# A fused attention and two-MoE kernel on one core: weight conversions on a timetable, second-MoE weights begun later, first stage reordered, state update ahead of output

## The chip, the cores and the metric

The kernel runs on one core of a Trainium2 chip. The metric is the time of one execution on the device, in microseconds (us). Other times here are us too, unless marked ns. The five engines of the core each work through their own list of instructions in order: TensorE (PE in the profile; its weight loads are PEld), VectorE (DVE), ScalarE (ACT), GpSimd (POOL) and SyncE (SP, which here issues nearly all transfers).

## The reference

```python
# attention: B, H, S, D = 4, 8, 768, 48
for t in range(S):
    state = alpha[:, :, t, :, None] * state + np.einsum('bhd,bhe->bhde', k[:, :, t], v[:, :, t])
    y[:, :, t] = np.einsum('bhd,bhde->bhe', q[:, :, t], state)
# x: 3072 tokens x 384
rms = np.sqrt(np.mean(x * x, axis=-1, keepdims=True) + 1e-06)
xn = x / rms * rms_g
g = xn @ w_gate                      # 384 x 1536
silu = g * (1.0 / (1.0 + np.exp(-g)))
x = (silu * (xn @ w_val)) @ w_out    # MoE 1
h = x @ w_in                         # 384 x 2048
out = (h * np.cos(h)) @ w_out2       # MoE 2
```

All is float32.

## The kernel before, in words

**Tiles and stages.** The 3072 tokens are cut into 8 blocks of 384 (`TT`). A block has four attention units, one per pair of heads (`units`, 32 in all; the pairs come in the order 3, 0, 1, 2). A unit is scanned (`att_prep`, five VectorE steps: `G`, a reciprocal `dr`, `q*G`, the backward scan, `k` scaled), transposed on PE (`att_T`, matrix `pt`, copied to `th` by ACT), scored (`att_sc0` or `att_sc`, matrices `ps`, copied by ACT and masked by POOL), and then updates the carried state (`att_u`: matrix `pu` needs `th`; VectorE makes `w` from it in three steps, L403 and L407) and gives its output (`att_y`: matrix `py`; the result goes to `xT`). The two last pairs' rows are put into their places by six small copies on SP (`att_fix`, L443 and L444). Then come the squares (`square`, `sq`), their sums over rows on PE (`rms_rows`, `rm`), nine VectorE steps for the inverse root (`rms_inv`, `ny` to `yb`), its spreading on PE (`rms_out`, `rb`, and `y`), and the split of the normed block into a high and a low part (`x_split` or `xn_write`, `xh` and `xl`).

**MoE 1** runs over 12 feature blocks `f` of 128 for each token block: nine matmuls for the gate (`m1_gate`, `pg`), Silu on ACT (`th<-pg`, L649), nine for the value (`m1_val`, `pv`), a product, and `hh` and `hl`, its high and low part; two feature blocks later nine matmuls add to the output (`m1_out`, `o`). Every matrix product takes three matmuls, high by high, high by low and low by high (`mm9`, L611). `pg` and `pv` share three buffers of PSUM, so the third such matrix must wait until the first has been read. For the first block the gate is multiplied by the inverse root afterwards (L647); for the others the input is already normed. MoE 2 follows with 6 blocks of 512 tokens and 16 feature blocks.

**Weights.** They arrive as 64-bit words' halves and must be converted: ACT takes two passes over the raw words (`assemble`, L166 and L168), VectorE joins them (`cv`, L169), ACT makes the high part (`split`, L78), VectorE the low part (L81). The weights of MoE 1 (`st_g`, `st_v`, `st_o` of 768 columns, later `ws` of 384) are converted during the first stage (pieces `a` and `b` of the string `FIRST`) and in the first token block, by `slot()`, which is called three times in each feature block and counts them in `step`. The weights of MoE 2 are loaded into three `ws` buffers (`pre2_stage`), converted from the second token block on (`pre2_conv`) and put back to memory.

**Order.** The work of the first stage is written out by `FIRST`: `p` prepares a unit, `T` transposes, `s` scores, `u` is the state update, `y` the output, `r` squares and row sums, `x` the split, `g` and `v` the first gate and value products, `n` and `o` the inverse root, `i` idle matmuls, `l` loads. Later attention is cut into pieces that a list (`stream`) hands out by `step`. The framework's scheduler then orders each engine's list; `tc.issue_after(x)` keeps what is inside from going ahead of instruction `x`, and `keep_in_program_order` holds an instruction in the place it was written. `slot()` ties a conversion to the Silu and the low part of the feature block before the last (`th_ins[-2]`, `hl_ins[-2]`), and the attention pieces to the end of the first stage (`held`):

```python
        if step[0] < 36 and (step[0] % 3 < 2 or step[0] > 12):
            a = th_ins[-2] if len(th_ins) > 1 else held[0][0]
            d = hl_ins[-2] if len(hl_ins) > 1 else held[0][1]
            with tc.issue_after(a), tc.issue_after(d):
                conv_piece()
            if 1 < streamed[0] and step[0] < NHOLD:
```

Of the kernel before, what the change touches and what calls it, by code (L numbers as in the profile page):

```python
# [42 lines left out]
WS = 2.0 ** 8  # L43
RSQRT_SEED = float(0x5F3759DF)
FIRST = (
    "p0 p1 T0 s0 u0 i3 p2 T1 s1 y0 u1 p3 T2 s2 y1 a0 u2 T3 s3 b0 a1 y2 l4 r0 r1 u3 b1 a2 x0 x1 y3 x2 "
    "g0 r2 b2 n0 v0 g1 o0 v1"
)


@with_exitstack
def fused_kernel(ctx: ExitStack, tc: tile.TileContext, akq, vin, wg, wv, wo, g_in, w2i, w2o, out):
# [100 lines left out]
    def done(eng, ins):  # L153
        mark[eng] = ins.ins
# [5 lines left out]
                st.enter_context(tc.issue_after(x))  # L160
            yield

    def assemble(st, v, pin=False):
        w = st.bitcast(I32).rearrange("p (n t) -> p n t", t=2)
        lo, hi = w[:, :, 0], w[:, :, 1]
        act.activation(out=lo, in_=lo.bitcast(U32), func=AF.Identity, scale=LOW_SCALE, bias=low)  # L166
        g = hi.bitcast(F32)
        done("act", act.activation(out=g, in_=g, func=AF.Prelu, scale=HIGH_SCALE, alpha=NEG_SCALE))  # L168
        ins = dve.scalar_tensor_tensor(  # L169
            out=v, in0=hi, scalar=3, in1=lo, op0=ALU.logical_shift_left, op1=ALU.bitwise_or  # L170
        )
        done("dve", ins)
        if pin:
            tc.keep_in_program_order(ins)
# [39 lines left out]
    def pre2_conv():  # L214
        if not pre2:
            return
        key, q, st = pre2.pop(0)
        if q == 0:
            w2s[key] = [dpool.tile([128, 1536], F32, name=f"d_{key}{x}") for x in "hl"]
        w = cv.tile([128, 2, 384], F32R, tag="whl", name="whl")  # L220
        h, l = w[:, 0, :], w[:, 1, :]
        v = cv_tile(st)
        assemble(st, v, True)
        split(h, l, v.bitcast(F32))
        for x, d in zip((h, l), w2s[key]):
            sp.dma_start(out=d[:, q * 384:(q + 1) * 384], in_=x.bitcast(F32))
        pre2_stage()
# [185 lines left out]
    def att_y(u):  # L413
        i, p = units[u]
        s = un[u]
        py = (ps_a if i else ps_g).tile([128, 512], F32, tag="a" if i else "g", name="py")
        cs = [slice(n * C, (n + 1) * C) for n in range(NB)]
        for n, c in enumerate(cs):
            for r0, r1, j in ((0, 64, 0), (64, R, 1)):
                pe.matmul(py[r0:r1, c], s["v"][:, n, r0:r1], s["s"][:, n, j, :], start=n == 0, stop=False)  # L420
        for n, c in enumerate(cs):
            if n >= 1 - i % 2:
                for r0 in (0, 64):
                    r = slice(r0, r0 + D)
                    done("pe", pe.matmul(  # L425
                        py[r, c], s["st"][n][r, :], s["q"][r, c], start=False, stop=n == NB - 1
                    ))
        if i not in xT:
            xT[i] = m1.tile([128, 4, TT], F32, tag="xT", name="xT")
        x = xT[i]  # L430
        if i:
            act.activation(out=x[:R, p, :], in_=py[:R, :TT], func=AF.Copy)
        else:
            done("act", act.activation(out=x[0:D, p, :], in_=py[0:D, :TT], func=AF.Copy))
            if u == 3:
                done("dve", dve.tensor_copy(out=x[64:R, p, :], in_=py[64:R, :TT]))
            else:
                done("act", act.activation(out=x[64:R, p, :], in_=py[64:R, :TT], func=AF.Copy))

    def att_fix(i):  # L440
        x = xT[i]
# [62 lines left out]
    def rms_out(i):  # L504
        yb = rms.pop(i)
        pb = ps_a.tile([128, 512], F32, tag="a", name="rb")
        done("pe", pe.matmul(pb[:, :TT], ones, yb.rearrange("p a c -> p (a c)"), start=True, stop=True))
        if i == 0:
            y = cv.tile([128, 2, TT], F32, tag="whl", name="y0")[:, 0, :]
        else:  # L510
            y = m1.tile([128, TT], F32, tag="y", name="y")
        done("act", act.activation(out=y, in_=pb[:, :TT], func=AF.Copy))
        rms[i] = y

    def rms_mm(i):
        rms_rows(i, 0, 1)
# [28 lines left out]
    def att_pieces(i):  # L545
# [8 lines left out]
                att_fix(i)  # L554

        if i == 0:
            def sums(c):
                square(0, c)
                rms_rows(0, c, 3)

            fn = dict(
                p=att_prep, T=att_T, s=att_sc0, u=att_u, y=y, a=lambda _: conv_a(), b=lambda _: conv_b(),
                x=x_split, r=sums, i=lambda n: keep_clock(n, ones), l=load_all,
                g=lambda f: pre_gate(f), v=lambda f: pre_val(f), n=lambda _: rms_inv(0), o=lambda _: rms_out(0),
            )
            return [(lambda k=k: fn[k[0]](int(k[1]))) for k in FIRST.split()]
# [13 lines left out]
                att_prep(u + 1)  # L580

        def E(u):
            y(u)
            if u + 1 < len(units):
                att_u(u + 1)
            if u + 2 < len(units):
                att_loadq(u + 2)
                att_loadv(u + 2)
# [26 lines left out]
                k += 1  # L615

    hid1 = {}
    th_ins = []
    hl_ins = []
    acc1 = {}  # L620

    pre = {}
# [17 lines left out]
    def m1_gate(i, f):  # L640
        if i == 0 and f < 2:
            pg = pre.pop(("g", f))
        else:
            pg = m1_mm(i, "g", f, ps_g.tile([128, 512], F32, tag="g", name="pg"))
        p = pg[:, :TT]
        if i == 0:
            dve.tensor_tensor(out=p, in0=p, in1=rms[0], op=ALU.mult)  # L647
        t = m1.tile([128, TT], F32, tag="t", bufs=4, name="th")
        th_ins.append(act.activation(out=t, in_=p, func=AF.Silu, scale=1.0 / WS).ins)  # L649
        return t  # L650

    def m1_val(i, f, t):
# [5 lines left out]
        hh = m1.tile([128, TT], F32R, tag="hh", bufs=3, name="hh")  # L658
        hl = m1.tile([128, TT], F32R, tag="hl", bufs=3, name="hl")
        dve.tensor_tensor(out=p, in0=t, in1=p, op=ALU.mult)  # L660
        copy_r(hh, p)
        hl_ins.append(sub_r(dve, hl, p, hh).ins)
        hid1[i, f] = (hh, hl)

    def m1_out(i, f):
# [276 lines left out]
```

## Time and profile before

| | |
|---|---|
| median of 3 runs | 1025.6 us (1021.43 to 1025.95) |
| the profiled execution | 1024.08 us |
| its span, first to last instruction | 1022.3 us |
| PE busy | 999.3 us, 98% of the span, 5870 matmuls |
| DVE, ACT, POOL busy | 533.9 us (52%), 559.7 us (55%), 178.1 us (17%) |
| mean granted clock of TensorE | 0.984 of full speed |
| chain of work that ended last | PE 92%, DMA 4%, DVE 2%, ACT 1% |

The span is the distance from the first to the last instruction of the profiled execution; 1.8 us of its own time lie around it. The busy shares are means over stages that differ: the first 41 us are attention and the conversion of the first weights, up to 125 us the first token block with the other conversions, up to about 570 us seven blocks of MoE 1 with attention beside them, and the rest is MoE 2. The granted clock is 1.00 at full speed (2.4 GHz) and 0.50 at half (1.2 GHz); a mean between them says how the stretch is shared. "Idle before" names what ended an engine's wait.

### The profile page before, as it was taken

The numbers are of one execution on the slowest core, as the hardware profiler recorded it, in microseconds if no ns is written. First come the engines' busy times: TensorE is split into PE (matmuls) and PEld (weight loads), VectorE is DVE, ScalarE is ACT, GpSimd is POOL, SyncE is SP. The second block draws the span as 40 slices with busy tenths as digits, with TensorE's granted clock in tenths as the row PEclk, the third lists the DMA queues.
The fourth block names the chain that finished last, engine by engine and source line by source line (L and its number), as shares of the span: only waits on it lengthen the run. The fifth ranks groups of instructions, "written<-read, shape, count | busy, mean of one in ns | idle before, by whom it ended". The sixth has DMA issues, their size and how long they took to land.

```text
span 1022.3 us, 15511 instructions
## 1 busy us (share of the span) xinstructions
PE 999.3 (98%) x5870; PEld 883.7 (86%) x5870; DVE 533.9 (52%) x1012; ACT 559.7 (55%) x1089; POOL 178.1 (17%) x189
## 2 busy tenths in 40 slices
PE   8799799999999999999999999999999999999998
PEld 6588799999999999999999998888888888888886
DVE  6879766666567666666625224343343333423333
ACT  4887545555455554554523226565575665755654
POOL 3010010000010000110000122233332233323331
PEclk7799899999999999999999999999999999999999
DMA  8736233343343353343311465010010000000000
GB/s 247 266 117 185 86 104 97 99 139 97 112 143 91 100 160 95 101 134 91 122 49 40 161 253 188 1 31 31 1 63 1 1 31 1 31 1 1 32 1 31
DMA packets 42795, 90.33 MB, mean 88 GB/s; under 512 B 5584, under 2 KB 25552, under 8 KB 42720
## 3 DMA queue, kind: packets, MB, share of 16 engines
q1 hardware_dynamic: 40416, 76.76, 24.5%
q0 software_dynamic: 2304, 12.58, 3.4%
q8 instruction: 46, 0.75, 0.3%
q14 instruction: 29, 0.24, 0.1%
HBM read 66.12 MB, written 22.02 MB: 86 GB/s over the span
## 4 chain that ended last, share of the span: by engine, by line
PE 92%; DMA 4%; DVE 2%; ACT 1%; SPq 0%; issue 0%; DVEq 0%; ACTq 0%
PE p L611 20%; PE ph L611 20%; PE o L611 15%; PE pv L611 14%; PE pg L611 14%; PE py L420 2%; DMA ak<-akq 2%; PE py L425 2%; PE pu L397 1%; DMA q<-akq 1%; PE ps L331 1%; PE ps L332 1%; PE ps L333 1%; DMA st_o<-wo 1%; PE pt L341 1%; PE ps L384 1%
## 5 line engine op out<-in xcount | busy, mean ns | idle before, releaser
L81 POOL TENSOR_TENSOR hl<-kk,hh 128x512 fp32r<-128x512 f32 x93 | 120.1, 1294 | 271.4 <-PE ph L611 105.8
L721 DVE SCALAR_TENSOR_TENSOR kk<-kk,ph 128x512 f32<-128x512 int32 x96 | 66.0, 688 | 142.4 <-ACT kk L720 141.7
L348 POOL TENSOR_SCALAR_AFFINE_SELECT sm<-sm 128x512 f32<-128x512 f32 (+1 forms) x64 | 45.4, 715 | 476.4 <-ACT sm L347 476.4
L724 DVE SCALAR_TENSOR_TENSOR kk<-kk,ph 128x512 f32<-128x512 f32 x96 | 65.9, 687 | 110.7 <-ACT kk L723 110.7
L660 DVE TENSOR_TENSOR pv<-th,pv 128x384 f32<-128x384 f32 x96 | 53.6, 558 | 78.1 <-PE pv L611 54.7
L720 ACT ACTIVATE kk<-ph 128x512 int32<-128x512 f32 x96 | 57.5, 599 | 65.7 <-PE ph L611 48.5
L649 ACT ACTIVATE th<-pg 128x384 f32<-128x384 f32 x96 | 46.7, 487 | 69.4 <-PE pg L611 64.2
L722 ACT ACTIVATE kk<-kk 128x512 f32<-128x512 f32 x96 | 60.6, 631 | 43.5 <-DVE kk L721 42.3
L78 ACT ACTIVATE hh<-kk 128x512 fp32r<-128x512 f32 x96 | 60.5, 631 | 42.9 <-DVE kk L724 38.1
L78 ACT ACTIVATE hh<-pv 128x384 fp32r<-128x384 f32 x96 | 46.9, 488 | 57.0 <-DVE pv L660 56.6
L81 DVE TENSOR_TENSOR hl<-pv,hh 128x384 fp32r<-128x384 f32 x96 | 53.3, 555 | 38.9 <-ACT hh L78 37.9
L723 ACT ACTIVATE kk<-kk 128x512 f32<-128x512 f32 x96 | 60.5, 630 | 2.4
L166 ACT ACTIVATE ws<-ws,low 128x384 int32<-128x384 uint32 x44 | 28.5, 649 | 54.8 <-DMA ws<-w2o 25.4
L78 ACT ACTIVATE bdh<-q 48x384 fp32r<-48x384 f32 x48 | 25.1, 523 | 40.5 <-DVE q L308 39.9
L308 DVE TENSOR_TENSOR q<-q,G 112x384 f32<-112x384 f32 x30 | 16.9, 564 | 42.2 <-DMA q<-akq 42.2
L611 PE MATMUL pv<-xh,v2h 128*128 128x384 f32 x96 | 32.9, 343 | 4.9 <-ACT th L649 4.9
L611 PE MATMUL pg<-xh,g0h 128*128 128x384 f32 x96 | 34.3, 357 | 0.1
L611 PE MATMUL pv<-xh,v1h 128*128 128x384 f32 x96 | 33.4, 348 | 0.8 <-ACT th L649 0.8
L611 PE MATMUL o<-hl,o0h 128*128 128x384 f32 x96 | 33.4, 348 | 0.5 <-DVE hl L81 0.5
L611 PE MATMUL pg<-xh,g1h 128*128 128x384 f32 x96 | 33.5, 349 | 0.0
L611 PE MATMUL o<-hl,o1h 128*128 128x384 f32 x96 | 33.5, 349 | 0.0
L611 PE MATMUL pg<-xl,g0h 128*128 128x384 f32 x96 | 33.0, 344 | 0.3 <-DVE xl L525 0.3
(241 smaller groups left out, 2963.1 us busy)
## 6 DMA issues: line engine op xcount, KB each, us to landing
ak<-akq SPq DMA_DIRECT2D x29, 337.8 KB, 3.6
ws<-w2i SPq DMA_DIRECT2D x16, 384.0 KB, 3.4
ws<-w2o SPq DMA_DIRECT2D x16, 384.0 KB, 3.3
v<-vin SPq DMA_DIRECT2D x32, 168.0 KB, 3.4
q<-akq SPq DMA_DIRECT2D x30, 168.0 KB, 3.2
x2d<-x SPq DMA_DIRECT2D x24, 192.0 KB, 2.0
x<-x2d SPq DMA_DIRECT2D x18, 256.0 KB, 2.8
out<-o SPq DMA_DIRECT2D x17, 256.0 KB, 2.3
```

Of the source, the lines that this page charges most:

```text
L78: return act.activation(out=dst, in_=src, func=AF.Copy)
L81: return eng.tensor_tensor(out=dst, in0=a, in1=h.bitcast(F32), op=ALU.subtract)
L166: act.activation(out=lo, in_=lo.bitcast(U32), func=AF.Identity, scale=LOW_SCALE, bias=low)
L348: pool.affine_select(out=dst, in_=dst, pattern=[[0, n], [1, C]], compare_op=ALU.is_ge, fill=0.0, base=0, channel_multiplier=-1,)
L611: pe.matmul(dst, w[a][:, cols(kc)], rhs[kc][b], start=first and k == 0, stop=last and k == 3 * len(rhs) - 1,)
L649: th_ins.append(act.activation(out=t, in_=p, func=AF.Silu, scale=1.0 / WS).ins)
L660: dve.tensor_tensor(out=p, in0=t, in1=p, op=ALU.mult)
L720: act.activation(out=kk, in_=ph, func=AF.Copy, scale=1.0 / (TWO_PI * WS))
L721: dve.scalar_tensor_tensor(out=r, in0=kk, scalar=-TWO_PI * WS, in1=ph, op0=ALU.mult, op1=ALU.add)
L722: act.activation(out=r, in_=r, func=AF.Sin, scale=0.5 / WS)
L723: act.activation(out=r, in_=r, func=AF.Square)
L724: dve.scalar_tensor_tensor(out=r, in0=r, scalar=-0.5, in1=ph, op0=ALU.add, op1=ALU.mult)
```

## The change

It has four parts. (1) `CONV` lists the steps at which `slot()` converts: 0, 1, 2, then every second step to 14, then each from 16 on; and `behind()` ties each conversion, those of MoE 2 too, to the Silu and the low part of the feature block that is current (`ahead`) instead of two earlier. (2) The three first loads of MoE 2's weights are asked for one feature block later, at `(1, 1)`, and its conversions lose `keep_in_program_order`. (3) `FIRST` is reordered: the splits `x` go before the squares (now `q`) and row sums (`r`), the pieces `a1`, `b1`, `a2`, `b2` stand later, each of the first four outputs is copied half by ACT and half by DVE (before, three of them wholly by ACT), and the first streamed piece, which prepares unit 4, is held like the others until the first stage's inverse root. (4) In `E(u)` the state update of the next unit is written ahead of the output of this one.

```diff
 FIRST = (
-    "p0 p1 T0 s0 u0 i3 p2 T1 s1 y0 u1 p3 T2 s2 y1 a0 u2 T3 s3 b0 a1 y2 l4 r0 r1 u3 b1 a2 x0 x1 y3 x2 "
-    "g0 r2 b2 n0 v0 g1 o0 v1"
+    "p0 p1 T0 s0 u0 i3 p2 T1 s1 y0 u1 p3 T2 s2 a0 y1 l4 u2 T3 s3 b0 y2 u3 x0 x1 a1 y3 x2 b1 g0 "
+    "q0 q1 q2 r0 r1 r2 n0 a2 v0 g1 b2 o0 v1"
 )
+CONV = {0, 1, 2, 4, 6, 8, 10, 12, 14} | set(range(16, 36))
...
-        assemble(st, v, True)
-        split(h, l, v.bitcast(F32))
+        with behind():
+            assemble(st, v)
+            split(h, l, v.bitcast(F32))
...
             done("act", act.activation(out=x[0:D, p, :], in_=py[0:D, :TT], func=AF.Copy))
-            if u == 3:
-                done("dve", dve.tensor_copy(out=x[64:R, p, :], in_=py[64:R, :TT]))
-            else:
-                done("act", act.activation(out=x[64:R, p, :], in_=py[64:R, :TT], func=AF.Copy))
+            done("dve", dve.tensor_copy(out=x[64:R, p, :], in_=py[64:R, :TT]))
...
         def E(u):
-            y(u)
             if u + 1 < len(units):
                 att_u(u + 1)
+            y(u)
...
+    @contextmanager
+    def behind():
+        a, d = ahead[0] if step[0] else held[0]
+        with tc.issue_after(a), tc.issue_after(d):
+            yield
...
     def slot():
-        if step[0] < 36 and (step[0] % 3 < 2 or step[0] > 12):
+        if step[0] in CONV:
             stage_w()
             if not todo or todo[0][0] == 2:
                 stage_tail()
-            a = th_ins[-2] if len(th_ins) > 1 else held[0][0]
-            d = hl_ins[-2] if len(hl_ins) > 1 else held[0][1]
-            with tc.issue_after(a), tc.issue_after(d):
+            with behind():
                 conv_piece()
         while stream and stream[0][0] <= step[0]:
             piece = stream.pop(0)[1]
-            streamed[0] += 1
-            if 1 < streamed[0] and step[0] < NHOLD:
+            if step[0] < NHOLD:
...
-        if i == 1:
-            for _ in range(NWS):
-                pre2_stage()
         for f in range(12):
+            if (i, f) == (1, 1):
+                for _ in range(NWS):
+                    pre2_stage()
```

`ahead[0]` is set at the end of `rms_out(0)` and then by each gate (its ACT part) and each value (both parts) of the feature blocks after `(0, 0)`. In the changed kernel most lines have numbers lower by one (L402 is L403 before, L434 is the DVE copy of L436, L431 is L432), from L432 to the MoE lower by two to five (L449 is L453, L480 is L484), and Silu is L650 for L649, the helpers `copy_r` and `sub_r` L79 and L82 for L78 and L81, the conversion L167, L169 and L170 for L166, L168 and L169.

What the scheduler makes of it, at three places. First, VectorE's list in the first stage, from the last step of unit 3's preparation (L305, tile `akq`) to the state update of unit 2 (`w`, `c_94`) and a little on; `G`, `dr`, `ak` and `q` without "kq" are unit 4's preparation (the trace calls the scans `TENSOR_TENSOR_SCAN`). Before:

```order
L305 TENSOR_TENSOR akq<-akq 112x384
L296 SCALAR_TENSOR_TENSOR G<-ak,d_91 112x387
L297 RECIPROCAL dr<-G 112x3
L169 SCALAR_TENSOR_TENSOR cv<-st_g_156 128x768
L403 TENSOR_TENSOR w<-pu,ge 112x144
L298 SCALAR_TENSOR_TENSOR ak<-ak,dr 112x387
L308 TENSOR_TENSOR q<-q,G 112x384
L407 SCALAR_TENSOR_TENSOR w<-w,ge 112x48
L305 TENSOR_TENSOR ak<-ak 112x384
L407 SCALAR_TENSOR_TENSOR c_94<-w,ge 112x48
L81 TENSOR_TENSOR g0l<-cv,g0h 128x768
L169 SCALAR_TENSOR_TENSOR cv<-st_v_160 128x768
```

Now, from the same step on:

```order
L304 TENSOR_TENSOR akq<-akq 112x384
L170 SCALAR_TENSOR_TENSOR cv<-st_g_156 128x768
L434 COPY xT<-py 48x384
L402 TENSOR_TENSOR w<-pu,ge 112x144
L406 SCALAR_TENSOR_TENSOR w<-w,ge 112x48
L406 SCALAR_TENSOR_TENSOR c_94<-w,ge 112x48
L82 TENSOR_TENSOR g0l<-cv,g0h 128x768
L434 COPY xT<-py 48x384
L402 TENSOR_TENSOR w<-pu,ge 112x144
L406 SCALAR_TENSOR_TENSOR w<-w,ge 112x48
L406 SCALAR_TENSOR_TENSOR c_95<-w,ge 112x48
```

The five steps of unit 4's preparation have left this piece (they come after the inverse root now), and a copy of each output (`xT<-py`) stands ahead of each state update.

Second, ScalarE's list at the head of the first token block, from `y`, the copy of the spread inverse root, to the first `th<-pt` of unit 4 (128x224). Before:

```order
L512 ACTIVATE y_478<-rb 128x384
L78 ACTIVATE ge<-G 112x3
L78 ACTIVATE v0h<-cv 128x768
L343 ACTIVATE th<-pt 128x224
L649 ACTIVATE th<-pg 128x384
L166 ACTIVATE st_o_494<-st_o_494,low 128x768
L168 ACTIVATE st_o_494<-st_o_494 128x768
L166 ACTIVATE st_g_498<-st_g_498,low 128x768
L168 ACTIVATE st_g_498<-st_g_498 128x768
```

Now:

```order
L508 ACTIVATE y_478<-rb 128x384
L167 ACTIVATE st_v_492<-st_v_492,low 128x768
L169 ACTIVATE st_v_492<-st_v_492 128x768
L167 ACTIVATE st_o_494<-st_o_494,low 128x768
L169 ACTIVATE st_o_494<-st_o_494 128x768
L79 ACTIVATE g0h<-cv 128x768
L650 ACTIVATE th<-pg 128x384 x2
L79 ACTIVATE ge<-G 112x3
L79 ACTIVATE v0h<-cv 128x768
L342 ACTIVATE th<-pt 128x224
```

Four passes over `st_v` and `st_o` now stand between `y` and the first two Silus (`th<-pg`), and the first `th<-pt` has moved behind those Silus.

Third, ScalarE's list at the end of the first token block; `ws` in the piece of before are MoE 2's first weights, in the piece of now the last of MoE 1's. Before:

```order
L343 ACTIVATE th<-pt 128x336
L78 ACTIVATE v2h<-cv 128x384
L78 ACTIVATE o2h<-cv 128x384
L432 ACTIVATE xT<-py 112x384
L166 ACTIVATE ws<-ws,low 128x384
L168 ACTIVATE ws<-ws 128x384
L166 ACTIVATE ws<-ws,low 128x384
L168 ACTIVATE ws<-ws 128x384
L453 ACTIVATE sq<-xT 128x384
L649 ACTIVATE th<-pg 128x384
```

Now:

```order
L449 ACTIVATE sq<-xT 128x384
L346 ACTIVATE sm<-ps 128x3x128
L342 ACTIVATE th<-pt 128x336
L79 ACTIVATE ge<-G 112x3
L431 ACTIVATE xT<-py 112x384
L449 ACTIVATE sq<-xT 128x384
L650 ACTIVATE th<-pg 128x384
L167 ACTIVATE ws<-ws,low 128x384
L169 ACTIVATE ws<-ws 128x384
```

MoE 2's passes have left; the order copy to `xT`, square (`sq`), Silu (`th<-pg`) is as it was. On PE the last output `py` of this block, which stood 18 large matmuls and a `pu` ahead of the value product `pv` that needs that Silu's buffer, stands directly ahead of it now, `pu` before it.

## Rows read from the trace of the kernel before

**Rows 1.** The page: span, and busy time of the engines.

```profile
span 1022.3 us, 15511 instructions
...
PE 999.3 (98%) x5870; PEld 883.7 (86%) x5870; DVE 533.9 (52%) x1012; ACT 559.7 (55%) x1089; POOL 178.1 (17%) x189
```

**Rows 2.** Waits of PE, whole span (us in total, times, longest us).

```profile
PE pv L611 <- ACT th L649: 5.7, 2, 4.9
PE pu L397 <- ACT th L343: 2.6, 2, 1.6
PE o L611 <- ACT hh L78: 1.8, 1, 1.8
...
PE pt L341 <- ACT sm L347: 1.0, 1, 1.0
PE o L611 <- DVE hl L81: 0.5, 1, 0.5
```

**Rows 3.** Stretches: us, busy us (instructions) of each engine, granted clock, DMA share, GB/s.

```profile
core 0: us, PE busy (x) PEld busy (x) DVE busy (x) ACT busy (x) POOL busy (x), PEclk, DMA share, GB/s
...
32.00:36.00 4.00, 3.65 (x20) 2.56 (x17) 3.75 (x7) 2.16 (x5) 0.00 (x0) 0.50 1.04 384
...
56.00:60.00 4.00, 4.00 (x19) 3.75 (x21) 3.12 (x5) 4.00 (x8) 0.00 (x0) 0.65 0.45 178
112.00:116.00 4.00, 0.16 (x1) 0.16 (x1) 1.66 (x3) 2.23 (x6) 0.00 (x0) 0.68 0.05 16
116.00:120.00 4.00, 4.00 (x19) 3.29 (x20) 3.76 (x8) 1.70 (x6) 0.00 (x0) 0.50 0.00 0
76.80:102.40 25.60, 25.60 (x190) 22.69 (x190) 23.14 (x50) 19.09 (x42) 1.04 (x2) 1.00 0.64 187
300.00:500.00 200.00, 199.87 (x1411) 189.53 (x1410) 131.13 (x277) 104.01 (x236) 15.99 (x23) 1.00 0.39 112
```

**Rows 4.** DVE, timeline of the first stage: start, us, instruction, [idle before <-releaser].

```profile
23.30 0.96 DVE L296 TENSOR_TENSOR_SCAN G<-ak,d 112x387 f32<-112x387 f32 x1 [2.29 <-DMA ak<-akq]
...
27.51 0.55 DVE L305 TENSOR_TENSOR ak<-ak 112x384 f32<-112x384 f32 x1
...
31.51 0.31 DVE L403 TENSOR_TENSOR w<-pu,ge 112x144 f32<-112x144 f32 x1 [1.54 <-PE pu L397]
...
35.26 0.56 DVE L436 COPY xT<-py 48x384 f32<-48x384 f32 x1
```

**Rows 5.** PE, timeline, end of the first stage and head of the first block.

```profile
41.53 0.88 PE L507 MATMUL rb<-yb,ones 128*128 128x384 f32 x2
...
46.61 0.44 PE L611 MATMUL pg<-xh,g0h 128*128 128x384 f32 x1
```

**Rows 6.** ACT, timeline, head of the first block.

```profile
46.45 1.00 ACT L166 ACTIVATE st_o<-st_o,low 128x768 int32<-128x768 uint32 x1
47.33 0.93 ACT L168 ACTIVATE st_o<-st_o 128x768 f32<-128x768 f32 x1
```

**Rows 7.** ACT, timeline, end of the first block.

```profile
108.82 0.47 ACT L432 ACTIVATE xT<-py 112x384 f32<-112x384 f32 x1
...
113.94 0.64 ACT L166 ACTIVATE ws<-ws,low 128x384 int32<-128x384 uint32 x1 [1.77 <-DMA ws<-w2i]
...
114.92 0.51 ACT L453 ACTIVATE sq<-xT 128x384 f32<-128x384 f32 x1
115.33 0.46 ACT L649 ACTIVATE th<-pg 128x384 f32<-128x384 f32 x1
```

**Rows 8.** PE, timeline, end of the first block.

```profile
105.84 0.60 PE L425 MATMUL py<-q,w 48*48 48x128 f32 x8
...
115.84 0.69 PE L611 MATMUL pv<-xh,v2h 128*128 128x384 f32 x1 [4.92 <-ACT th L649]
```

**Rows 9.** Copies to xT issued at 109.3 to 109.9 us (KB, us to landing).

```profile
xT<-xT SPq DMA_DIRECT2D x1, 24.0 KB, 5.1
```

**Rows 10.** The same for those issued at 79.3 to 80 us.

```profile
xT<-xT SPq DMA_DIRECT2D x1, 24.0 KB, 2.1
```

More of the change, by code (lines that the diff above doesn't have):

```diff
@@ L161, in in_order, with assemble @@
             yield
-    def assemble(st, v, pin=False):
+    def assemble(st, v):
         w = st.bitcast(I32).rearrange("p (n t) -> p n t", t=2)
@@ L168, in assemble @@
         done("act", act.activation(out=g, in_=g, func=AF.Prelu, scale=HIGH_SCALE, alpha=NEG_SCALE))
[L169 removed]
+        done("dve", dve.scalar_tensor_tensor(
             out=v, in0=hi, scalar=3, in1=lo, op0=ALU.logical_shift_left, op1=ALU.bitwise_or
[L171 to L174, printed above, removed]
+        ))
     def split(h, l, f):
@@ L513, in rms_out @@
         rms[i] = y
+        if i == 0:
+            ahead[0] = (mark["act"], mark["dve"])
     def rms_mm(i):
@@ L556, in att_pieces @@
         if i == 0:
-            def sums(c):
-                square(0, c)
-                rms_rows(0, c, 3)
             fn = dict(
                 p=att_prep, T=att_T, s=att_sc0, u=att_u, y=y, a=lambda _: conv_a(), b=lambda _: conv_b(),
-                x=x_split, r=sums, i=lambda n: keep_clock(n, ones), l=load_all,
+                x=x_split, q=lambda c: square(0, c), r=lambda c: rms_rows(0, c, 3), i=lambda n: keep_clock(n, ones), l=load_all,
                 g=lambda f: pre_gate(f), v=lambda f: pre_val(f), n=lambda _: rms_inv(0), o=lambda _: rms_out(0),
@@ L617, in fused_kernel @@
     hid1 = {}
-    th_ins = []
-    hl_ins = []
+    ahead = {}
+    step = [0]
+    @contextmanager
[3 more added lines that the diff above has]
+            yield
     acc1 = {}
@@ L648, in m1_gate @@
         t = m1.tile([128, TT], F32, tag="t", bufs=4, name="th")
-        th_ins.append(act.activation(out=t, in_=p, func=AF.Silu, scale=1.0 / WS).ins)
+        a = act.activation(out=t, in_=p, func=AF.Silu, scale=1.0 / WS).ins
+        if (i, f) > (0, 0):
+            ahead[0] = (a, ahead[0][1])
         return t
@@ L660, in m1_val @@
         dve.tensor_tensor(out=p, in0=t, in1=p, op=ALU.mult)
-        copy_r(hh, p)
-        hl_ins.append(sub_r(dve, hl, p, hh).ins)
+        a, d = copy_r(hh, p).ins, sub_r(dve, hl, p, hh).ins
+        if (i, f) > (0, 0):
+            ahead[0] = (a, d)
         hid1[i, f] = (hh, hl)
@@ L805, in fused_kernel @@
             stream.append((36 * (j - 1) - LEAD + n * 34 // len(p), x))
-    step = [0]
-    streamed = [0]
     def slot():
-        if step[0] < 36 and (step[0] % 3 < 2 or step[0] > 12):
+        if step[0] in CONV:
             stage_w()
```

## The prediction

> **What bounds the kernel now.** I read the page's shares first: PE is busy for 999.3 of 1022.3 us, so 23 us are all that waits can give back [rows 1]. The list of PE's waits says what ends them: Silu (`th<-pg`) for `pv`, twice, 4.9 us the longest; `th<-pt` for `pu`, 1.6 the longest and the other 1.0; `hh`, `sm` and `hl` once each, 1.8, 1.0 and 0.5 [rows 2]. Then the stretches tell where they lie. From 300 to 500 us PE is busy for 199.87 of 200 at a granted clock of 1.00: nothing there can become shorter by a better order. The losses lie before 125 us, in idle time and in stretches at the half level (1.2 GHz): 32 to 36 us at 0.50, 56 to 60 at 0.65, 112 to 116 with PE at work for 0.16 us, and 116 to 120 at 0.50, behind that idle time [rows 3]. So I go through the first 125 us piece by piece; the rest is PE's own work, of which the change alters nothing but the order.
>
> **A. First stage, to the spreading `rb`.** VectorE is the engine that others wait for here. It stands 2.29 us for the transfer of unit 4's `ak`, at 23.30, and then spends the five steps of unit 4's preparation, of which the first, at 23.30, takes 0.96 and the last, at 27.51, 0.55 us, and all five 3.6 of the 4.8 between, ahead of unit 3's state update at 31.51 [rows 4]. In the new list these steps come after the inverse root. Ahead of the update of unit 3 there are instead two more output copies of 0.56 [rows 4], 1.1 together. So unit 3's update comes 2.3 + 3.6 - 1.1 = 4.8 us earlier. From it to `rb`, at 41.53 [rows 5], it is 10.0 us now. There the splits go ahead of the squares, one conversion of `st_o` leaves ahead of the root, and the squares come later; I leave the 10.0 as it is, so `rb` falls at 36.7. Bounds: 2.3 if the conversion pieces, later in the list, make VectorE wait where the transfer did; 6.3 if the 1.54 us that it waits for `pu` at 31.51 [rows 4] go too. I take 4.8: **-4.8** (-6.3 to -2.3).
>
> **B. Head of the first token block.** ScalarE's new list has four conversion passes between `y` and the first Silu, where it had one `th` and a split. Such passes take 1.00 and 0.93 us [rows 6], in a row some 3.6, and no attention piece is there yet to fill PE. The third product needs the buffer that this Silu reads, so PE stands. Against the present order, in which the gate behind that wait comes at 46.61, 5.1 us after `rb` [rows 5], I make it 3.2 more, since the one `th` that stood there took its 0.4 too. In exchange ScalarE has those passes behind it, and the later waits of this stretch, for `sm` (1.0) and `hh` (1.8) [rows 2], shrink to some 1.2 of their 2.8: -1.6. Sum **+1.6**; between -1.0 (other transposes and scores fill PE) and +3.2 (the later waits stay).
>
> **C. 45 to 60 us.** The 0.5 us wait for `hl` [rows 2] goes, since the low part of the step before no longer stands behind a conversion, and with it the stretch at 0.65, which costs 4 x 0.35 = 1.4 us plus its edges, 1.7 in all [rows 3]: -2.2. But unit 4's preparation has now come here, where, to judge by the stretch from 76.8, VectorE is busy for 23.1 of 25.6 us [rows 3]: of its 3.6 us I let a third show, +1.2. Sum **-1.0** (-2.2 to +1.4).
>
> **D. End of the first token block.** ScalarE copies the last output to `xT` only at 108.82, then takes two conversions of MoE 2's first weights, the second waiting 1.77 us for its transfer, before the square at 114.92 and the Silu at 115.33 [rows 7]. PE had given that output by 106.4, and its `pv` waits 4.92 until 115.84 [rows 8]; the 4 us at 0.50 behind it cost 2.0 and the edges 0.1: 7.0 in all. The copy that puts the last pair's rows in place was issued behind the weights' loads and landed after 5.1 us [rows 9]; one at 79 us took 2.1 [rows 10]. With the change the two conversions leave ScalarE's list there. Yet the last `py` now stands directly ahead of this `pv`, so PE has nothing between them, and the chain stays: copy 0.47, landing 2.1, square 0.51, Silu 0.46 [rows 7, 10], 3.5 us of wait. The half-clock stretch behind I scale with the wait, 2.1 x 3.5/4.9 = 1.5. So 5.0 for 7.0: **-2.0**. Bounds: the landing at 5.1 gives 6.5 + 2.1 = 8.6, that is +1.6; a chain hidden wholly, -7.0. I take 2.1, because most of the loads ahead of the copy at 109 us are asked for later now. The Trainium skill (DMA: Bandwidth & Descriptors, section "Anatomy of one DMA — SWDGE (gpsimd) path") gives a transfer 2.0 us fixed plus its bytes over 436 GB/s; estimated by that page the 24 KB copy takes 2.06 wherever it stands, and the wait would be 3.5 by it. Its fit is for transfers issued by GpSimd, this one is issued by SP, and at this very place the trace disagrees, with 5.1.
>
> **E. Seven further blocks and MoE 2.** In each later unit `pu` of the next unit now stands directly ahead of `py`, and the conversions of MoE 2 follow the current feature block. PE has no waits there [rows 3], and VectorE (131 of 200 us) and ScalarE (104) have room to absorb the four instructions that shift per unit. The last stages' lists do not change. I put **+0.5** for stray waits (0 to +14, see the second rival).
>
> **Sum:** -4.8 + 1.6 - 1.0 - 2.0 + 0.5 = -5.7 us against the profiled execution's own 1024.08, so 1018.4, told as **1018**. That execution lies 1.5 us, 0.15%, under the median of the runs shown, 1025.6. About 0.5%, 5.1 us, is what a measurement of this kernel can tell from no change; the forecast lies barely beyond it. The forecast's own range, with its terms' bounds not all at one end, is 1012 to 1023.
>
> **Rivals.**
> *The end of the first block stays as long (no change).* MoE 2's loads are moved by one feature block, but two of the three still stand ahead of the next units' `k`, `v`, `q` loads and that copy on SP, so the change would not do there what it says. For it: the 5.1 us [rows 9], and `py` directly ahead of `pv`. Against it: the first of those loads and ScalarE's two conversions are out of the way in any case. D is then +1.6 for -2.0, 3.6 more: 1022.
>
> *`pu` ahead of `py` makes PE wait in every unit (slower).* `pu` needs ScalarE's copy `th`; asked for earlier, it may come before the copy is there, and PE's list has no other work until it is. The price is that of the two waits of this kind in the trace, 1.0 and 1.6 us [rows 2], on some 28 streamed units. Against it: between `pt` and `pu` there are still some 22 matmuls, 3.1 us at the 0.14 us that one takes from 300 to 500 us (199.87/1411), while a `th` takes 0.46 [rows 3, 7]; and nothing waits there today [rows 3]. It decides from 5.7/28 = 0.2 us a unit, where the gain is gone, and 0.39 makes the kernel slower by over 0.5%. At 0.5 a unit: +14, so 1032.
>
> *The clock stays full (a larger gain).* Behind denser work in the first stage PE may be granted 1.00 where it had 0.50 from 32 to 36 us, worth half of the 3.65 us that it was busy [rows 3], 1.8; and a shorter wait in D may leave no half-clock stretch behind it, 1.5: 1018.4 - 1.8 - 1.5 = 1015. For it: the two stretches follow idle time and partly idle PE [rows 3]. Against it: in 56 to 60 us the clock fell after idle times much shorter than the 3.5 us that stay in D.
>
> **How the numbers follow.** The forecast gets 0.48, and of its range three quarters lie beyond 0.5%: 0.36 faster, 0.12 the same. The first rival gets 0.25, all the same. The second gets 0.13, slower, since the distance between `pt` and `pu` speaks against it but every unit would pay. The third gets 0.14, faster. Together: faster 0.50, the same 0.37, slower 0.13. The range reaches from 1010, for the third rival with A at its best, to 1028, for the first rival with B and C at their worst or the second at 0.35 us a unit; the rest of the second, about one in ten, and the tails beside it stay outside.
>
> **What would show it.** A is right if `rb` stands near 36.7 us and unit 3's update near 26.7; wrong if VectorE's wait of 2.3 us has come back before it. B is right if ScalarE's four passes stand between `y` and the first Silu and PE shows one wait of about 3 us for `th<-pg` or for the buffer behind it; wrong if PE is busy there. C is right if no half-clock stretch lies between 45 and 60 us. D is right if no conversion of MoE 2's weights stands in ScalarE's list before the Silu of the last feature block and PE's wait ahead of `pv` is about 3.5 us; wrong from 4.9. The second rival shows as waits of `pu` on `th`, or `py` on `w`, repeated between 130 and 570 us. The whole prediction falls if PE's total idle time of 23 us has not gone down by at least 3.

## The result, and the profile after

The changed kernel takes **1016.28 us** (median of 4 runs, 1015.18 to 1017.27) against 1025.61 beside it: a ratio of 0.9918, with an interval of 0.989 to 0.9946. That is faster by 0.8%, inside the range of 1010 to 1028 and 2 us under the 1018 forecast. The profiled execution takes 1016.89, 7.2 less than the one of before.

The page of the changed kernel answers to [rows 1]:

```profile
span 1015.2 us, 15535 instructions
...
PE 993.6 (98%) x5870; PEld 882.8 (87%) x5870; DVE 538.1 (53%) x1015; ACT 557.0 (55%) x1086; POOL 178.1 (18%) x189
```

PE stood idle for 23.0 us and now stands for 21.6. Waits thus gave back only 1.4 of the 7.2 us by which the profiled execution is shorter; the rest is less busy time, with the same 5870 matmuls. Its waits (us in total, times, longest) say what took the place of [rows 2]:

```profile
PE pv L605 <- ACT th L650: 3.9, 1, 3.9
PE pg L605 <- ACT th L650: 3.4, 1, 3.4
PE pg L605 <- ACT xh L522: 2.9, 2, 1.8
```

The 4.9 us before `pv` is 3.9. At the head of the first block the waits for `th<-pt`, `sm`, `hh` and `hl` have given way to one of 3.4 us for the Silu. Those for `xh` are new and lie in the first stage. Stretches, columns as in [rows 3]:

```profile
44.00:48.00 4.00, 3.26 (x15) 2.15 (x16) 4.00 (x9) 2.68 (x7) 0.00 (x0) 0.52 0.52 143
48.00:52.00 4.00, 4.00 (x15) 3.78 (x15) 4.00 (x7) 3.43 (x6) 0.52 (x1) 0.50 0.32 98
52.00:56.00 4.00, 4.00 (x18) 3.53 (x17) 3.57 (x7) 1.34 (x3) 0.00 (x0) 0.70 0.95 353
56.00:60.00 4.00, 4.00 (x26) 3.97 (x24) 2.46 (x4) 4.00 (x8) 0.52 (x1) 1.00 0.58 208
112.00:116.00 4.00, 3.29 (x16) 2.86 (x17) 3.91 (x9) 3.62 (x9) 0.00 (x0) 0.57 0.00 0
116.00:120.00 4.00, 3.31 (x24) 2.85 (x22) 3.69 (x12) 0.77 (x3) 0.00 (x0) 1.00 0.35 98
300.00:500.00 200.00, 200.00 (x1435) 191.05 (x1435) 135.08 (x280) 104.75 (x238) 14.54 (x22) 1.00 0.39 116
```

The half-clock stretch at 56 us is gone, but one from 44 to 54 us stands behind the new wait; the one at the end of the block is shorter. From 300 to 500 us PE is as fully busy as it was, yet 1435 of its matmul records fall into these 200 us instead of 1411. A stretch that looked full has become shorter.

Where the time went shows when the kernel is cut at three marks on PE, the first spreading `rb`, the `rb` of the next block (`rb1`) and the first product of MoE 2:

| us | to `rb` | `rb` to `rb1` | `rb1` to MoE 2 | MoE 2 to the end |
|---|---|---|---|---|
| before | 41.5 | 83.1 | 488.5 | 409.1 |
| changed | 38.8 | 83.2 | 483.5 | 409.7 |
| difference | -2.7 | 0.0 | -5.0 | +0.5 |

The two middle columns as stretches, columns as in [rows 3], before:

```profile
41.53:124.66 83.13, 73.56 (x490) 64.83 (x490) 69.19 (x135) 59.94 (x121) 5.87 (x8) 0.94 0.45 140
124.66:613.21 488.55, 487.64 (x3361) 464.74 (x3361) 287.55 (x597) 227.07 (x510) 42.08 (x64) 1.00 0.38 114
```

and after:

```profile
38.80:121.97 83.17, 74.96 (x490) 66.73 (x490) 72.07 (x141) 59.75 (x119) 6.02 (x8) 0.92 0.48 149
121.97:605.51 483.54, 483.54 (x3360) 463.81 (x3360) 290.49 (x597) 228.96 (x516) 42.15 (x64) 1.00 0.38 116
```

Two thirds of the gain lie between `rb1` and MoE 2, in the part for which I had put +0.5; PE does the same work there in 4.1 us less busy time, and waits 0.9 us less.

### The profile page after: what moved, and what is told of

It is laid out like the page before. It is cut to its first block, busy times and chain, and to the rows that moved or that the text cites. A ratio compares the mean times of both kernels' runs of the same rounds, so it can differ in the third digit from the quotient of the medians.

```text
span 1015.2 us, 15535 instructions
## 1 busy us (share of the span) xinstructions
PE 993.6 (98%) x5870; PEld 882.8 (87%) x5870; DVE 538.1 (53%) x1015; ACT 557.0 (55%) x1086; POOL 178.1 (18%) x189
## 4 chain that ended last, share of the span: by engine, by line
PE 95%; DMA 3%; ACT 1%; DVE 0%; issue 0%; SPq 0%; DVEq 0%; ACTq 0%
PE p L605 20%; PE ph L605 20%; PE pv L605 15%; PE pg L605 15%; PE o L605 15%; PE py L419 2%; PE py L424 2%; DMA ak<-akq 2%; PE pu L396 1%; PE ps L330 1%; PE ps L331 1%; PE ps L332 1%; PE ps L383 1%; PE pt L340 1%; PE rb L503 1%; DMA q<-akq 0%
## 5 line engine op out<-in xcount | busy, mean ns | idle before, releaser
L82 POOL TENSOR_TENSOR hl<-kk,hh 128x512 fp32r<-128x512 f32 x93 | 120.2, 1295 | 271.4 <-PE ph L605 105.8
L79 ACT ACTIVATE hh<-pv 128x384 fp32r<-128x384 f32 x96 | 47.0, 490 | 98.9 <-DVE pv L663 98.6
L79 ACT ACTIVATE hh<-kk 128x512 fp32r<-128x512 f32 x96 | 60.5, 631 | 42.7 <-DVE kk L728 37.9
L650 ACT ACTIVATE th<-pg 128x384 f32<-128x384 f32 x96 | 46.8, 488 | 65.2 <-PE pg L605 59.8
L82 DVE TENSOR_TENSOR hl<-pv,hh 128x384 fp32r<-128x384 f32 x96 | 53.2, 554 | 26.0 <-ACT hh L79 25.2
L346 ACT ACTIVATE sm<-ps 128x512 f32<-128x512 f32 (+1 forms) x64 | 30.5, 483 | 15.9 <-PE ps L332 14.2
L79 ACT ACTIVATE bdh<-q 48x384 fp32r<-48x384 f32 x48 | 25.1, 523 | 22.8 <-DVE q L307 22.0
L605 PE MATMUL pv<-xh,v0h 128*128 128x384 f32 x96 | 34.3, 357 | 0.0
L605 PE MATMUL pg<-xh,g0l 128*128 128x384 f32 x96 | 34.2, 356 | 0.0
L295 DVE TENSOR_TENSOR_SCAN G<-ak,d 112x387 f32<-112x387 f32 x30 | 30.6, 1022 | 6.4 <-DMA ak<-akq 5.8
L605 PE MATMUL pv<-xl,v0h 128*128 128x384 f32 x96 | 33.9, 353 | 0.0
```

Of the source, the lines that this page charges most:

```text
L79: return act.activation(out=dst, in_=src, func=AF.Copy)
L82: return eng.tensor_tensor(out=dst, in0=a, in1=h.bitcast(F32), op=ALU.subtract)
L295: dve.tensor_tensor_scan(Gf, a[:, 0:n], d1.rearrange("p n c -> p (n c)"), 0.0, ALU.mult, ALU.add)
L605: pe.matmul(dst, w[a][:, cols(kc)], rhs[kc][b], start=first and k == 0, stop=last and k == 3 * len(rhs) - 1,)
L650: a = act.activation(out=t, in_=p, func=AF.Silu, scale=1.0 / WS).ins
```

## The experiments

**Which part gives the 5 us.** Theory G: it is PE's order of `pu` and `py`, by the switches between tile shapes. Theory C: it is the conversions' timetable.

*Part 4 undone in the changed kernel:*

```diff
         def E(u):
+            y(u)
             if u + 1 < len(units):
                 att_u(u + 1)
-            y(u)
```

> The changed kernel with the output written ahead of the next unit's state update again (part 4 undone, all else kept). Theory G (grouping on PE): the gain behind the first block is the switch between PE's tile shapes. In the changed kernel 27 units have pu and py adjacent, pu first, and pu and the first part of py share the 128x64 shape; here, by the lists, 20 units have py then pu (0.15 us more each) and some 7 have them apart, with large matmuls between (about 0.4 more each): from the spreading rb of block 1 to the first product of MoE 2 483.5 + 20 x 0.15 + 7 x 0.4 = 489 us, and in all about 1022 to 1023. Rival theory C (the conversions' timetable unblocks the later blocks): that stretch stays at 483.5 to 484.5 and the time at 1016 to 1017.

Measured: 1026.91 us, ratio 1.0021 (1.0009 to 1.0033): all of the gain is gone, and the kernel is slower than before. `rb1` to MoE 2 takes 491.9 us. G holds in kind, and its price was too low, 489 for this stretch and 1022 to 1023 in all: beside the separated pieces PE also waits for `hl` five times, 2.3 us in all:

```profile
PE pg L605 <- DVE hl L82: 2.3, 5, 0.8
```

*Part 4 alone, in the kernel before:* the same edit the other way round.

> The kernel before with part 4 alone: the state update written ahead of the output. Theory G: its 22 adjacent pairs and 4 to 7 separated ones become 27 pairs with pu first, so from rb of block 1 to MoE 2 it takes 488.5 - 22 x 0.15 - 5 x 0.4 = about 483 to 484.5 us, and in all about 1020 to 1022 against 1025.6. Theory C: 488.5 stays, and the time stays within 1 us of 1025.6.

Measured: 1021.54 us, ratio 0.9968 (0.9951 to 0.9984); `rb1` to MoE 2 takes 484.1 us, `rb` to `rb1` 83.5. As G expects: of the 5.0 us, 4.4 come with this part alone. The parts don't add: alone it gives 3.3 us, and without it the other three lose 2. The order is what decides: in all twelve kernels here with `pu` first, whatever else was altered, `rb1` to MoE 2 takes 483.1 to 485.1 us, in the two with `py` first 488.5 and 491.9. Theory C falls with that.

What it saves is read from one unit of each kernel on PE's timeline. Before:

```profile
302.13 0.33 PE L611 MATMUL o<-hh,o0l 128*128 128x384 f32 x1
302.39 0.87 PE L420 MATMUL py<-sm,v 128*64 128x128 f32 x12
303.19 0.64 PE L425 MATMUL py<-q,w 48*48 48x128 f32 x8
303.76 0.55 PE L397 MATMUL pu<-v,th 128*64 128x48 f32 x12
304.24 0.44 PE L611 MATMUL pg<-xh,g1h 128*128 128x384 f32 x1
```

The changed kernel, the same number of matmuls:

```profile
299.74 0.34 PE L605 MATMUL pv<-xh,v1l 128*128 128x384 f32 x1
300.01 0.49 PE L396 MATMUL pu<-v,th 128*64 128x48 f32 x11
300.32 0.28 PE L419 MATMUL py<-sm,v 128*48 128x128 f32 x1
300.34 0.22 PE L396 MATMUL pu<-v,th 128*64 128x48 f32 x1
300.40 0.83 PE L419 MATMUL py<-sm,v 128*64 128x128 f32 x11
301.16 0.64 PE L424 MATMUL py<-q,w 48*48 48x128 f32 x8
301.73 0.44 PE L605 MATMUL o<-hh,o0h 128*128 128x384 f32 x1
```

The figures ahead of the operand shapes are the piece of the PE array that is used. From the large matmul ahead to the one behind it was 302.13 to 304.24, 2.11 us, and is 299.74 to 301.73, 1.99. Before, the shape changed four times (128 to 64, to 48, back to 64, back to 128 columns); now `pu` runs straight into the first part of `py`, which has its shape, and there are three changes. Over all full units I count what a group adds, so that a delay of the first large matmul behind it is in it too: from the start of the large matmul ahead to that of the second one behind, less two large ones at 0.174 us. The median saving is the same: 0.13 us for a pair (2.05 to 1.92 with 20 and 12 matmuls, 2.15 to 2.02 with 24 and 8). Where large matmuls had stood between `py` (1.57) and `pu` (0.68), two more changes go: 2.24 to 1.92, 0.32. In the trace of before 19 full pairs were adjacent and some 4 units apart: 19 x 0.13 + 4 x 0.32 = 3.8 of the 4.1 us that the stretches around small matmuls lost between the two marks; the other 0.9 us are waits between large matmuls. `ps` and `pt` (112 rows, 128 columns) show no such price: three, six and nine `ps` cost 0.36, 0.72 and 1.08. That the order gives the 5 us is shown by the two runs; that the changes of shape are the reason is read from these starts, since no run altered the shapes alone.

**The first stage.** *The old first stage in the changed kernel* (old `FIRST`, the three outputs copied by ScalarE again, unit 4's preparation let in):

```diff
-    "... T2 s2 a0 y1 l4 u2 T3 s3 b0 y2 u3 x0 x1 a1 y3 x2 b1 g0 q0 q1 q2 r0 r1 r2 n0 a2 v0 g1 b2 o0 v1"
+    "... T2 s2 y1 a0 u2 T3 s3 b0 a1 y2 l4 r0 r1 u3 b1 a2 x0 x1 y3 x2 g0 r2 b2 n0 v0 g1 o0 v1"
...
-            if step[0] < NHOLD:
+            streamed[0] += 1
+            if 1 < streamed[0] and step[0] < NHOLD:
```

> The changed kernel with the first stage of before (old order of its work, outputs copied as before, unit 4's preparation let into the first stage again). If what the first stage gave is passed on: rb back from 38.8 to about 41.5 us and the whole time 2 to 3.5 us longer, 1018.5 to 1020. Rival: the wait at the head of the first block, 3.4 us for the Silu, absorbs it (its conversions would be done while PE is still in the first stage): wait near 1 us, time unchanged at 1016 to 1017.

Measured: 1018.88 us, ratio 0.9935 (0.9911 to 0.9958), whose interval overlaps that of the change. The median lies in the range of the first expectation (1018.5 to 1020). The profiled execution points the other way: `rb` comes at 40.7, 1.9 us later, but `rb1` at 122.5 for 122.0 and the span ends within 0.1 us; the Silu's wait at the head is gone, and one of 3.0 us for `th<-pt` stands there. But this is the fastest of the four executions (1016.84; the others took 1018.69 to 1019.32), so whether the first block absorbs what the first stage gives stays open.

**The conversions.** *MoE 1's old timetable in the changed kernel:*

```diff
...
-        if step[0] in CONV:
+        if step[0] < 36 and (step[0] % 3 < 2 or step[0] > 12):
...
-            with behind():
+            a = th_ins[-2] if len(th_ins) > 1 else held[0][0]
+            d = hl_ins[-2] if len(hl_ins) > 1 else held[0][1]
+            with tc.issue_after(a), tc.issue_after(d):
                 conv_piece()
```

> The changed kernel with the conversions of MoE 1's weights on the old timetable (old steps, tied to the Silu and low part two feature blocks back); MoE 2's weights, first stage and update order stay as changed. If the new timetable costs at the head what I read there: one split only stands between y and the first Silu, PE's 3.4 us wait for th is under 0.5 us, and the half-clock stretch from 44.6 to 54.2 us (about 4.8 us lost) shrinks, so the time falls by 4 to 8 us to 1008 to 1012. Rival: the old timetable brings back waits for hh and sm in 45 to 60 us (2.8 us and the stretch at 0.65 in the kernel before), so that the sum stays within 2 us of 1016.

Measured: 1017.81 us, ratio 0.9929 (0.9908 to 0.9951). The rival holds, though with other waits than it named: the one for the Silu stays at 3.3 us and one of 3.3 us for a converted weight is added, so that `rb` to `rb1` takes 87.0 us:

```profile
PE pv L605 <- ACT v0h L79: 3.3, 1, 3.3
```

*MoE 2's weights as before in the changed kernel:*

```diff
...
-        with behind():
-            assemble(st, v)
-            split(h, l, v.bitcast(F32))
+        assemble(st, v, True)
+        split(h, l, v.bitcast(F32))
...
+        if i == 1:
+            for _ in range(NWS):
+                pre2_stage()
         for f in range(12):
-            if (i, f) == (1, 1):
-                for _ in range(NWS):
-                    pre2_stage()
```

> The changed kernel with MoE 2's weights as before (part 2 undone: first loads asked for at the start of block 1, conversions not tied to the current feature block, their VectorE step kept in the written place); the timetable of MoE 1's conversions, first stage and update order stay as changed. Theory D (ScalarE's conversions of MoE 2 and their loads stretch the wait at the end of the first block): two such conversions stand ahead of the last squares again, the wait of pv for the Silu goes from 3.9 to 5 or more, and the time rises by 1.5 to 4 us to 1018 to 1020. Rival: the chain copy, landing, square, Silu sets the wait by itself, which stays at 3.9 within 0.3, and the time at 1016 to 1017.5.

Measured: 1018.9 us, ratio 0.9942 (0.9927 to 0.9957). The time lies in the range of theory D (1018 to 1020), and the wait at the end of the block stays at 3.9 us, as the rival has it. The 2.6 us that the time seems to rise are thus not where D put them: `rb` to `rb1` takes 84.7 us for 83.2, and the stretch behind 485.1 for 483.5. But the run doesn't make the case that D needed: ScalarE runs the two conversions from 103.8 to 106.3 us, ahead of the copy to `xT` at 109.3 and not between it and the square, as it did before. What they would cost there stays open.

**The head of the first block.** *The conversions of steps 1 and 2 tied behind the first Silu:*

```diff
-        if (i, f) > (0, 0):
-            ahead[0] = (a, ahead[0][1])
+        ahead[0] = (a, ahead[0][1])
```

> The changed kernel with the conversions of steps 1 and 2 tied to the first feature block's Silu instead of to y, so that only a split stands between y and the first Silu on ScalarE. Theory B (the order at the head is the loss): PE's 3.4 us wait for th falls under 1 us, the half-clock stretch behind it (44.6 to 54.2) shrinks, the time falls by 3 to 6 us to 1010 to 1013. Rival (ScalarE's and VectorE's conversion work in 37 to 60 us is the loss, in whatever order): a wait for v0h, hh or hl of 2 to 4 us takes its place within the next feature blocks, as the one of 3.3 us for v0h did with the old timetable, and the time stays within 2 us of 1016.

Measured: 1014.1 us, ratio 0.9895 (0.988 to 0.9909). The wait of 3.4 us is 1.1, and one of 1.9 for `g0l` is new; `rb` to `rb1` takes 81.1 us, 2.0 less. The time falls by 2.2 us, less than the 3 to 6 of B and just beyond the 2 of its rival: the order at the head costs some 2 us. That the conversion work keeps the rest isn't shown.

*Idle matmuls in the wait:*

```diff
-    "... g1 b2 o0 v1"
+    "... g1 b2 o0 v1 i9 i5"
...
-        t = ps_o.tile([128, 512], F32, tag="o2", name="idle")
+        t = ps_o.tile([128, 512], F32, tag="o0" if "rb" in held else "o2", name="idle")
...
```

> The changed kernel with 14 idle matmuls (ones by ones, some 3.1 us of PE by the 0.224 us that one takes in the first stage) behind the second value product, where PE waits 3.4 us for the Silu; nothing else moves. Theory K (the half-clock stretch from 44.6 to 54.2 us hangs on that idle time, and is the larger part of what the head costs): the wait shrinks to about 0.3 us, the granted clock stays at 1.00 behind it, and up to 9.6/2 = 4.8 us come back: 1011 to 1013.5. Rival (ScalarE and VectorE set the pace of those feature blocks, so a faster PE only waits for them): new waits of PE for hh, th or split weights take the place, and the time stays within 1.5 us of 1016.

Measured: 1014.02 us, ratio 0.9904 (0.9887 to 0.9921). The idle matmuls, and the stretches of this kernel, columns as above:

```profile
40.50 3.61 PE L463 MATMUL idle<-ones 128*128 128x128 f32 x28
...
44.00:48.00 4.00, 3.77 (x26) 2.71 (x26) 4.00 (x9) 2.92 (x9) 0.00 (x0) 1.00 0.63 203
48.00:52.00 4.00, 4.00 (x25) 3.63 (x24) 4.00 (x10) 3.16 (x6) 2.82 (x2) 1.00 0.30 77
52.00:56.00 4.00, 4.00 (x25) 3.96 (x24) 4.00 (x7) 3.92 (x8) 0.00 (x0) 1.00 1.02 380
```

With PE at work through the wait the clock stays at 1.00 where it had 0.52, 0.50 and 0.70: K holds for the clock. Of the 4.8 us that K hoped for, `rb` to `rb1` gets back 3.0 (80.2 for 83.2): PE, now faster, waits for others again, 2.3 us for a `th<-pt` and 4.8 at the block's end:

```profile
PE pv L606 <- ACT th L651: 4.8, 1, 4.8
PE pu L396 <- ACT th L342: 2.8, 3, 2.3
```

**The end of the first block.** *The squares behind the Silu:*

```diff
-            stream.append((36 * (j - 1) - LEAD + n * 34 // len(p), x))
+            s = 36 * (j - 1) - LEAD + n * 34 // len(p)
+            stream.append((max(s, SQ) if j == 1 and n >= len(p) - 3 else s, x))
...
-        for c in range(3):
-            square(i, c)
+        with tc.issue_after(ahead[0][0]):
+            for c in range(3):
+                square(i, c)
```

with `SQ = 28`.

> The changed kernel with the squares of block 1 handed out three steps later and tied behind the Silu of feature block 9, so that ScalarE reaches that Silu without waiting for the small copies into xT. Theory D': pv's wait of 3.9 us at 108.8 goes (under 0.5), with the half-clock stretch behind it (some 1.5): the time falls by 3 to 5.5 us to 1011 to 1013.5. Rival: the row sums (rm) or the inverse root then wait as long a little later, since the copies still take 2.4 us: the time stays within 1.5 us of 1016.

Measured: 1017.45 us, ratio 0.9933 (0.9913 to 0.9952). The rival holds: the wait has only moved to the row sums. The profile puts it down to VectorE's `dr`, which ended last; what the row sums take is VectorE's sum of the squares, which ends at 115.8 us, behind a last square that could start only at 113.9, once the copies had landed:

```profile
115.94 0.55 PE L474 MATMUL rm<-sq,ones 128*32 128x96 f32 x8 [3.51 <-DVE dr L297]
```

*Both edits, first Silu and squares:*

> Both edits of e5 and e6 at once. If theories B and D' hold and the two places are independent, their gains add: 1005 to 1009 us. If the conversion work is the limit (the rivals), what is won at one place is waited for at the other: 1013 to 1016.

Measured: 1014.45 us, ratio 0.9903 (0.9876 to 0.9929): what the head's edit gives alone, and far from the 1005 to 1009 of two gains that add.

*The small copies early,* block 1's outputs being written in two halves:

```diff
-            if u == u0 + (3 if i else 0):
+            if u == u0 + (3 if i > 1 else 0):
...
-        if i:
+        if i > 1:
             act.activation(out=x[:R, p, :], in_=py[:R, :TT], func=AF.Copy)
+        elif i:
+            act.activation(out=x[0:D, p, :], in_=py[0:D, :TT], func=AF.Copy)
+            dve.tensor_copy(out=x[64:R, p, :], in_=py[64:R, :TT])
```

> The changed kernel with block 1's outputs written to xT in two pieces (ScalarE rows 0 to 47, VectorE rows 64 to 111, as block 0 does), so that the small copies from the last pair can be issued after that block's first output instead of its last. Theory D'' (the 2.4 us landing of those copies is the part of the chain that can be taken away): pv's wait at the end of the first block falls from 3.9 to about 1.5 us (copy 0.5, square 0.5, Silu 0.5), with some of the half-clock stretch, so the time falls by 2.5 to 4 us to 1012 to 1014. Rival (what the tail gains is waited for at the inverse root, as when the squares were moved): within 1.5 us of 1016.

Measured: 1016.76 us, ratio 0.9932 (0.9915 to 0.9949). The landing of the copies is off the chain, and VectorE's half of the output, queued behind its scans, has come in its place; `pv` waits 4.5 us. ScalarE's timeline:

```profile
109.15 0.47 ACT L433 ACTIVATE xT<-py 48x384 f32<-48x384 f32 x1
111.47 0.52 ACT L452 ACTIVATE sq<-xT 128x384 f32<-128x384 f32 x1 [1.85 <-DVE xT L434]
```

*With the head's edit:*

> The edit that ties the second conversions behind the first Silu (alone 1014.1 us) together with the early small copies. If the two places are independent: 1014.1 less 2.5 to 4, 1010 to 1011.5. If the tail's gain is waited for later: 1013.5 to 1014.5.

Measured: 1014.26 us, ratio 0.9907 (0.9892 to 0.9921): nothing is added. *And with 13 idle matmuls* (`i5 i8`):

> The last one and 13 idle matmuls (2.9 us) behind the second value product, where with that edit PE waits 1.1 and 1.9 us. Theory K: the clock stays at 1.00 from 42 to 56 us, 2 to 5 us less than without them: 1006 to 1009. Rival (VectorE, fully busy there, sets the pace): within 1.5 us of the kernel without them.

Measured: 1015.83 us, ratio 0.9922 (0.9907 to 0.9937). The clock is 1.00 from 40 to 48 us but falls to 0.67 in 52 to 56, behind a wait of 1.2 us for `sm`; theory K's gain doesn't show on top of the other edit. The idle matmuls and the head's edit, each alone, thus lie 2 us under the changed kernel, at 1014.0 and 1014.1; the ratios' intervals overlap with that of the change, so that they are better is likely and not settled.

## Why the prediction was right, point by point

The total was right to 2 us, and its terms were not. A to D were to give 6.2 us and gave 2.7, E was to cost 0.5 and gave 4.5: errors of 3.5 and 5.0 us stood against each other, and nothing in the prediction ties one to the other. That the number came out is luck. By its own last sign the prediction falls: PE's idle time was to go down by at least 3 of 23 us and went down by 1.4. The lower end of its range doesn't follow from its words either: the third rival's 1015 with A at its best is 1013.6, not 1010.

- **A, the first stage: -4.8 forecast, -2.7 measured.** Unit 3's update came even earlier than forecast. VectorE's timeline after, answering to [rows 4]:

```profile
24.75 0.31 DVE L402 TENSOR_TENSOR w<-pu,ge 112x144 f32<-112x144 f32 x1
...
26.95 1.15 DVE L523 SCALAR_TENSOR_TENSOR xl<-xT,g_sb,xh 128x384 fp32r<-128x384 f32 x2 [1.28 <-ACT xh L522]
29.16 0.96 DVE L170 SCALAR_TENSOR_TENSOR cv<-st_v 128x768 int32<-128x768 int32 x1 [1.05 <-ACT st_v L169]
...
34.63 0.21 DVE L481 TENSOR_SCALAR ny<-nm 128x96 int32<-128x96 int32 x1 [1.55 <-ACT nm L480]
```

  31.51 became 24.75, 6.8 less. The step that failed is "I leave the 10.0 as it is": from there to `rb` it takes 14.1 us now. VectorE, once it was early, waits for ScalarE, three times for 3.9 us in these rows, and `rb` itself stands in PE's list behind the second gate. The 2.7 us are those of one trace: in the eleven kernels here with the new first stage `rb` falls at 37.3 to 39.3 us, each time later than the 36.7 forecast.
- **B, the head: +1.6 forecast.** The wait of about 3 us was named and is there, 3.44 ahead of `pg`, and so are ScalarE's four passes between `y` and the Silu:

```profile
39.65 0.49 ACT L508 ACTIVATE y<-rb 128x384 f32<-128x384 f32 x1
40.03 1.00 ACT L167 ACTIVATE st_v<-st_v,low 128x768 int32<-128x768 uint32 x1
...
42.58 0.87 ACT L169 ACTIVATE st_o<-st_o 128x768 f32<-128x768 f32 x1
43.35 0.83 ACT L79 ACTIVATE g0h<-cv 128x768 fp32r<-128x768 f32 x1
44.09 0.85 ACT L650 ACTIVATE th<-pg 128x384 f32<-128x384 f32 x2
```

```profile
38.80 0.81 PE L503 MATMUL rb<-yb,ones 128*128 128x384 f32 x2
...
44.61 0.69 PE L605 MATMUL pg<-xh,g0h 128*128 128x384 f32 x1 [3.44 <-ACT th L650]
```

  What I left out is the clock behind it. **C, -1.0 forecast,** failed for the same reason: the short stretch at 56 us went, and one of 9.8 us, from PE's start at 44.6 to 54.4, came, worth up to 4.9. The idle matmuls show that this stretch hangs on that wait. Between `rb` and `rb1` PE stood idle for 8.2 us instead of 9.6, but by the edges of the granted clock it was at work at the half level for 12.7 us instead of 7.3, which costs 2.7 more.
- **D, the end of the block: a wait of 3.5 us forecast, 3.88 measured,** by the chain that was named. ScalarE after, answering to [rows 7]:

```profile
108.88 0.49 ACT L431 ACTIVATE xT<-py 112x384 f32<-112x384 f32 x1
111.75 0.52 ACT L449 ACTIVATE sq<-xT 128x384 f32<-128x384 f32 x1 [2.38 <-DMA xT<-xT]
112.18 0.47 ACT L650 ACTIVATE th<-pg 128x384 f32<-128x384 f32 x1
```

  The copy (issued at 109.6 us) lands after 2.0 us here, as at 79 us in [rows 10], so the first rival, with 5.1, falls:

```profile
xT<-xT SPq DMA_DIRECT2D x1, 24.0 KB, 2.0
```

  By the Trainium skill (DMA: Bandwidth & Descriptors, "Anatomy of one DMA — SWDGE (gpsimd) path") an estimate for it was 2.06; this row agrees, and the 5.1 of [rows 9] doesn't. My reason for taking 2.1, that MoE 2's loads are asked for later, is not borne out: in the kernel before with part 4 alone, which asks for them as before, the copy, then issued at 113.5 us, lands after 2.1 and `pv` waits 4.1; with part 2 undone in the changed kernel it is 2.1 and 3.9. The rows of the run with part 4 alone, of its transfers and of its waits:

```profile
xT<-xT SPq DMA_DIRECT2D x1, 24.0 KB, 2.1
PE pv L611 <- ACT th L649: 4.1, 1, 4.1
```

  B, C and D together were to give -1.4 and gave 0.0 by the marks.
- **E, the later blocks and MoE 2: +0.5 forecast, -4.5 measured, -5.0 of it before MoE 2. This is the step that failed most.** I had looked there for waits only, and from PE busy for 199.87 of 200 us [rows 3] I read that "nothing there can become shorter by a better order". But a busy engine's time also holds the switches between its instructions. A sign of it stood in the trace of before: `py` with `pu` apart cost 2.24 us and adjacent 2.05, by the same starts that show the saving now. The second rival had the right place and the wrong sign: `pu` ahead of `py` makes PE wait nowhere from 300 to 500 us, and shortens every unit. The Trainium skill (TensorEngine Tiling (Array Packing), section "Key Properties") says that a change of the tiling mode, not only of the tile, drains TensorE; it gives no price. The traces agree for the narrow pieces (64 and 48 columns): 0.13 us with one change fewer, 0.32 with two.
- **The third rival** (the clock stays full) didn't come about: the clock from 32 to 36 us is 0.50 as before, and 0.57 from 112 to 116, behind D's wait. Where it did stay full, at the head, it took work in the wait.

## What to carry to other kernels

Where an engine is busy all the time, its order can still be worth something: set the starts of its instructions beside each other and ask what a group of odd shape costs alone, next to its like and apart. Put matmuls that use the same piece of the PE array next to each other, above all in a pattern that repeats. And where several engines share a stretch that is full of work, a wait that is taken away at one place tends to come back at the next: measure to a mark well behind it, not at the wait.

## What the runs showed of the hardware that was not expected

Read from the starts of PE's matmuls, a change between tile shapes costs 0.13 to 0.16 us where columns are narrowed, and nothing between 112 and 128 rows. Some 3.6 us of idle matmuls in a 3.4 us wait kept the granted clock at 1.00 for the 16 us behind it, in which it had been at 0.50 for about ten.
